# Half of the first MLP layer as a Strassen product, with its token sums on GpSimd

## The chip, the cores and the metric

The kernel runs on one core of one Trainium2 chip. The metric is the time of one execution on the device in microseconds (us); the runs of a kernel are given by their median. A profile shows one execution, taken by the hardware profiler. PE is TensorE (PEld its weight loads), DVE is VectorE, ACT is ScalarE, POOL is GpSimd, SP is SyncE, which here only issues DMAs.

## The reference

Attention with 4 sink tokens and a window of 128, on 4 batches, 8 heads, 768 positions and head size 64, then layer normalisation and a two-layer MLP with a residual, on tokens of 512 values and 2048 hidden units. All inputs and the output are f32.

```python
keep = is_sink | in_window
scores = np.where(keep, scale * q @ k.T, -1e9)
a = softmax(scores)
x = (a @ v) with the heads side by side          # 4 x 768 x 512
xn = (x - mu) / np.sqrt(var + 1e-6) * g_ln
out = x + np.maximum(xn @ w_ch1, 0.0) @ w_ch2    # 512 -> 2048 -> 512
```

## The kernel before, in words

**Work.** A chunk is 256 tokens (two tiles of 128), three to a batch, twelve in all. `chunk` loads q, k and v of a chunk and brings q and k into transposed form (`kq`), from the fifth chunk on by plain loads into `nat` on POOL's queue (L659) and DMA transposes on SP's queue (L660 with L551). `attend` makes the scores in two halves (matmuls L763), the exponentials on ACT (L777), the mask multiply on DVE (L781), and `value` the products with v (L800, L805). `value` goes on with the normalisation on DVE and POOL: reciprocal (L818), x (L820), its statistics (L824, L826), the inverse square root on POOL (L832, L833), the normalised tile xc (L835) and its DMA transpose into `xnt` on SP (L845).

**The MLP.** `mlp` makes the first layer of a chunk in eight blocks of 128 x 512 results, each of 8 matmuls with 256 columns (L880), that is two groups of 128 hidden units for 256 tokens. In the first two chunks a block has one tile of tokens and 16 matmuls with 128 columns (L873). ACT or DVE evicts a block with its relu (L890, L892) into `hq`. From the third chunk on the second layer is a Strassen-Winograd product in `wino`: sums of quarters of the hidden values on DVE (L943), seven products of 8 matmuls each (L960), and sums out of the banks on DVE (L974, L981). PSUM has two pairs of banks for the attention and four single banks (`one`) for everything else. Sums of w2's quarters are made once (L1029).

**Order.** Nothing is issued in the order of the text. Each step is put to a planner (`Plan.op`) with the engines that may do it, a cost on each and a priority in units of time (chunk c's MLP has T = 16 c + 8; the steps of its attention are offsets in `PAR`). `Plan.run` goes through time on its own model of the engines, picks the ready step with the lowest priority on the engine that is free first, and gives buffers of a ring (`nat`, `x`, `pe`, ...) as they come free. From 40 units on, TensorE's steps keep strictly to the order of their priorities. What comes out is one fixed list, issued under a manual schedule; on the chip each engine runs its share in that order and waits on semaphores where the data ask for it. POOL's queue holds both its arithmetic and its loads. A load of chunk c is tied to the square root of chunk c - 3 (`behind`).

```python
def behind(c):
    return [roots[2 * (c - 3) + 1]] if c >= PAR["behind"] else []
...
P.op(f"{nm}ld{c}{i}", {"POOL": (0.87, 0.9)}, ld + 0.01 * i + 0.1 * x,
     lambda e, nat=nat, ap=ap: G.dma_start(nat.t, ap), writes=[nat], dma=SW, after=behind(c))
```

Of the kernel before, what the change touches and what calls it, by code (L numbers as in the profile page):

```python
# [7 lines left out]
FP32 = mybir.dt.float32  # L8
# [56 lines left out]
class Plan:  # L65
# [6 lines left out]
    LANES = 8  # L72
    SHARED = 36.0

    def __init__(self):
# [37 lines left out]
    def run(self):  # L113
# [8 lines left out]
        while ready:  # L122
# [50 lines left out]
            if o.dma is None:  # L173
                o.end = st + lat
            else:
                busy, first, last = o.dma
                q = "POOL" if e == "POOL" else "HW"
                at = max(st + occ + first, dma_free[q], dma_free["all"] if st < self.SHARED else 0.0) + busy
                dma_free[q] = dma_free["all"] = at
                o.end = at + last  # L180
                lanes[q][n_dma[q] % self.LANES] = o.end
                n_dma[q] += 1
# [29 lines left out]
def fix(occ, extra=0.09):  # L212
    return (occ, occ + extra)
# [9 lines left out]
HW_T = (0.10, 0.8, 0.8)  # L223

LOW, HIGH = 1e-9, 1e9
NEG = -1e30
NEVER = -1e9

PAR = dict(split=(3, 4, 5, 6, 7), gsum=-8.0, guard=183.0, strict=40.0, win=0.4, tr=-8.0, sc=-5.3, sc1=-2.0, av=2.0, trx=9.0, by_dma=4, x_by_dma=2, g_on_w=2, av2=20.0, avi=1.0, behind=5, gtt=9.0, ramp=0.3, vs0=2.6, vpb=12.0,
           w1p=(0.15, 1.7, 2.05, 2.8), pm=2, w2p=(4.5, 4.51, 4.52, 4.53), by_tile=2, wino=2, vp=(0.0, 0.1, 2.0, 2.1, 4.2, 4.3), ld1=0.05)  # L230

# [130 lines left out]
def kernel(  # L362
# [12 lines left out]
    nc = tc.nc  # L375
# [21 lines left out]
    def ring(name, n, shape, dtype, pool=consts):  # L397
        P.ring(name, [Slot(pool.tile(shape, dtype, name=f"{name}{i}"), f"{name}{i}") for i in range(n)])
# [10 lines left out]
    ring("kq", 4, [128, HP, 2, 256], BF16)  # L409
    ring("pe", 12, [128, 2, 512], BF16)  # L410
    ring("ps", 3, [128, 256], BF16)
    ring("kts", 2, [128, HP, 32], BF16)
    ring("x", 16, [128, DM], BF16)
    ring("xc", 6, [128, DM], BF16)
    ring("xnt", 4, [128, NDM, 256], BF16)
    ring("hq", 8, [128, 4, 512], BF16)
    ring("hs", 10, [128, 2, 2, 128], BF16)
    ring("tm", 6, [128, 256], FP32)
    ring("ot", 4, [128, DM], FP32)
# [116 lines left out]
    def at(c, step):  # L536
        return 16.0 * c - 8.0 + PAR[step]

# [15 lines left out]

    def behind(c):
        return [roots[2 * (c - 3) + 1]] if c >= PAR["behind"] else []

    def load_v(t, prio):
        b, r = t // RB, t % RB
        bv = Buf(f"v{t}", "vn")  # L560
        vn_b[t] = bv
        P.op(f"vld{t}", {"POOL": (0.87, 0.9)}, prio, lambda e: G.dma_start(  # L562
            bv.t[:, :, 0:64], v[b, :, 128 * r:128 * (r + 1), :].rearrange("h p d -> p h d")),
            writes=[bv], dma=SW, after=list(ones_of.values()) + behind(t // 2))
# [13 lines left out]
    def chunk(c):  # L578
# [74 lines left out]
        else:  # L653
            for x, (nm, src) in enumerate((("k", k), ("q", q))):
                for i in range(2):
                    nat = Buf(f"{nm}n{c}{i}", "nat")
                    ap = src[b, :, 256 * R + 128 * i:256 * R + 128 * (i + 1), :].rearrange("h p d -> p h d")
                    P.op(f"{nm}ld{c}{i}", {"POOL": (0.87, 0.9)}, ld + 0.01 * i + 0.1 * x,
                         lambda e, nat=nat, ap=ap: G.dma_start(nat.t, ap), writes=[nat], dma=SW, after=behind(c))  # L659
                    P.op(f"tr{nm}{c}{i}", {"SP": (1.2, 1.2)}, d + 0.01 * i, lambda e, nat=nat, i=i, x=x: dma_t(  # L660
                        T.t[:, :, x, 128 * i:128 * i + 128], nat.t.rearrange("p h d -> p (h d)")),
                        reads=[nat], writes=[T], dma=HW_X, after=[scores[c - 1]])
# [75 lines left out]
    def attend(c):  # L738
# [48 lines left out]
        for i in range(2):  # L787
            def part(h, n, i=i):
                col = 256 * i + 128 * n if R else 128 * (i + n)
                return pes[h // 2].t[:, h % 2, col:col + 128]  # L790
            value(c, i, pes, ps, (PAR["av2"] if c == 2 else at(c, "av")) + PAR["avi"] * i, part, [2 * c + i - 1, 2 * c + i] if R or i else [2 * c])

    def value(c, i, pes, ps, d, part, srcs):
# [3 lines left out]
        def av(e):  # L797
# [5 lines left out]
            for h in range(H):  # L803
# [13 lines left out]
        recs.append(rcb)  # L817
        P.op(f"rc{t}", {"DVE": fix(0.115)}, d + 0.1, lambda e: V.reciprocal(rc(), pv()[:, :, :, 64]),  # L818
             reads=[po], writes=[rcb])
        P.op(f"x{t}", {"DVE": dve(512)}, d + 0.11, lambda e: V.tensor_tensor(  # L820
            x.t.rearrange("p (a h c) -> p a h c", a=2, c=64), pv()[:, :, :, 0:64],
            rc().unsqueeze(3).to_broadcast([128, 2, 4, 64]), op=ALU.mult), reads=[po, rcb], writes=[x])
        mv = Buf(f"mv{t}")
        P.op(f"bn{t}", {"DVE": fix(0.60)}, d + 0.12, lambda e: V.bn_stats(st.t[:, 8:14], x.t),  # L824
             reads=[x], writes=[st, mv])
        P.op(f"ag{t}", {"DVE": fix(0.09)}, d + 0.13, lambda e: V.bn_aggr(st.t[:, 14:16], st.t[:, 8:14]),  # L826
             reads=[st], rw=[mv])
        rs = Buf(f"rs{t}")
        xst_b[t, "rs"] = rs
        scaled = c >= PAR["wino"]  # L830
        roots[t] = P.op(f"rs{t}", {"POOL": (0.83, 0.88)}, d + (0.5 if scaled else 5), lambda e: (
            G.tensor_scalar(st.t[:, 17:18], st.t[:, 15:16], 1e-6, None, op0=ALU.add),  # L832
            G.tensor_tensor(st.t[:, 16:17], st.t[:, 17:18], mhalf, op=ALU.pow)),  # L833
            reads=[st, mv, Bc["mhalf"]], writes=[rs])
        P.op(f"xc{t}", {"DVE": fix(0.26)}, d + (0.6 if scaled else 0.14), lambda e: V.tensor_scalar(  # L835
            xc.t, x.t, st.t[:, 14:15], st.t[:, 16:17] if scaled else None, op0=ALU.subtract,
# [7 lines left out]
        if c >= PAR["x_by_dma"]:  # L844
            P.op(f"trx{t}", {"SP": (1.2, 1.2)}, d + 0.5, lambda e: dma_t(xnt_b[c].t[:, :, 128 * i:128 * i + 128], xc.t),  # L845
                 reads=[xc], writes=[xnt_b[c]], dma=HW_X)
            return
# [5 lines left out]
        if c >= PAR["g_on_w"]:  # L853
# [5 lines left out]
            reads=[pt, Bc["gt"]], writes=[xnt_b[c], xnt_t[t]])  # L859

    def mlp(c):
        T = 16.0 * c + 8.0
# [3 lines left out]
        hq = [Buf(f"hq{c}_{g}", "hq") for g in range(2)]  # L866
        for u in range(NH1 // 2):
            ph, hb, hg = Buf(f"ph{c}_{u}", "one"), Buf(f"h{c}_{u}"), hq[u // 4]
# [7 lines left out]
            def mm(e, u=u, ph=ph):  # L876
                for s in range(2):
                    ht = 2 * u + s
                    for j in range(NDM):
                        nc.tensor.matmul(ph.t[:, 256 * s:256 * s + 256],  # L880
                                         lhsT=w1[ht // 4][:, j, 128 * (ht % 4):128 * (ht % 4 + 1)],
                                         rhs=xnt.t[:, j, :], start=j == 0, stop=j == NDM - 1)
            pr = T + u + 0.5
            o = P.op(f"ph{c}_{u}", pe(0.872), pr, mm_t if by_tile else mm, reads=[xnt_t[2 * c + u % 2] if by_tile else xnt, (Bw1 if c < PAR["g_on_w"] else Bw1g)[u // 2]],
# [11 lines left out]
        if c >= PAR["wino"]:  # L896
            return wino(c, T, hq, h1)
        for i in range(2):
# [27 lines left out]

    def wino(c, T, hq, h1):
        A = [lambda g=g: hq[g].t.rearrange("p (v k) (s t) -> p k v s t", k=2, s=2) for g in range(2)]
        part = {"a11": lambda g: A[g]()[:, 0, :, :, 0:128], "a21": lambda g: A[g]()[:, 0, :, :, 128:256],
                "a12": lambda g: A[g]()[:, 1, :, :, 0:128], "a22": lambda g: A[g]()[:, 1, :, :, 128:256]}  # L930
        deps = {n: [h1[4 * g + (0 if n[2] == "1" else 1)::2][:2] for g in range(2)] for n in part}
        sb = {}
# [6 lines left out]
        for i, (n, x0, x1, op) in enumerate((("s3", "a11", "a21", ALU.subtract), ("s1", "a21", "a22", ALU.add),  # L939
                                             ("s2", "s1", "a11", ALU.subtract), ("s4", "a12", "s2", ALU.subtract))):  # L940
            for g in range(2):
                sb[n, g] = Buf(f"{n}_{c}{g}", "hs")
                P.op(f"{n}_{c}{g}", {"DVE": dve(512, 0.52)}, T - 4 + 4 * g + 0.2 * i, lambda e, n=n, x0=x0, x1=x1, g=g, op=op: V.tensor_tensor(  # L943
                    sb[n, g].t, get(x0, g), get(x1, g), op=op),
                    reads=need(x0, g) + need(x1, g), writes=[sb[n, g]], hold=[hq[g]])
# [25 lines left out]
        def keep(name, r, done, half, pr):  # L971
            tm[name] = Buf(f"tm{name}{c}", "tm")
            i, sl = half // 2, slice(256 * (half % 2), 256 * (half % 2) + 256)
            return P.op(f"tm{name}_{c}", {"DVE": dve(256, 1.14)}, pr, lambda e: V.tensor_tensor(  # L974
                tm[name].t, at(r), xs[i].t[:, sl], op=ALU.add), reads=[done, xs[i]], hold=[bank[reg[r][0]]], writes=[tm[name]])
        oo = {}

        def final(r, done, name, half, pr):
            i, sl = half // 2, slice(256 * (half % 2), 256 * (half % 2) + 256)
            oo[half] = Buf(f"oo{c}{half}")  # L980
            return P.op(f"o{c}_{half}", {"DVE": dve(256, 1.14)}, pr, lambda e: V.tensor_tensor(  # L981
                ots[i].t[:, sl], at(r), tm[name].t, op=ALU.add), reads=[done, tm[name]], hold=[bank[reg[r][0]]], writes=[ots[i], oo[half]])
# [49 lines left out]

    for c in range(NC):
        mlp(c)
        if c == PAR["g_on_w"] - 1:
# [93 lines left out]
```

## Time and profile before

| what | value |
|---|---|
| three runs shown | 210.74, 211.32, 211.52 us (median 211.32) |
| the profiled execution's own time | 211.71 us |
| its span, first to last instruction | 210.2 us |
| PE, DVE, ACT, POOL busy | 203.0, 162.2, 114.1, 83.5 us |
| granted TensorE clock | 1.000 |
| chain that ended last | PE 90%, DMA 3%, DVE 3%, POOL 2% |
| matmuls of layer one, L880 | 640, 74.5 us busy |
| matmuls of layer two, L960 | 320 with `hs`, 240 with `hq` weights |

The span is what the trace covers; about 1.5 us lie around it. Matmuls run in a pipeline: a row's mean (273 ns for L880) is the time from start to finish of one, while the next starts after 109 ns, so a block's length is read from the chain or the timeline and not from the mean. On DVE and ACT a queued instruction starts about 0.1 us before the one ahead has ended. A group's idle time is what its engine waited just before it.

### The profile page before, as it was taken

To read this page: it belongs to the slowest core of one execution; us is meant where nothing else is said; L and a number is where in the kernel's file an instruction comes from. 1 tells how busy PE (TensorE), PEld (TensorE's weight loads), DVE (VectorE), ACT (ScalarE), POOL (GpSimd) and SP (SyncE) were. 2 spreads that over 40 slices of the span, in tenths; PEclk is the share of its full clock that TensorE was granted. 3 is DMA by queue.
4 is the path that set the end of the run, shared out by engine and by line. 5 is a ranking of instruction groups with operands and counts; after the bars stand their busy time and mean duration, and the time that the engine had idled before them with its cause. 6 is when DMAs were issued, how large, how long until landed. Compare 5 with 4: busy or idle time off the path is not lost.

```text
span 210.2 us, 6259 instructions
## 1 busy us (share of the span) xinstructions
PE 203.0 (97%) x2539; PEld 167.9 (80%) x2544; DVE 162.2 (77%) x410; ACT 114.1 (54%) x168; POOL 83.5 (40%) x126
## 2 busy tenths in 40 slices
PE   6978999999999999999999999999999999999994
PEld 2657997764787997997987987987988988988883
DVE  5579759999688688798687797797787786797353
ACT  2559479837564564564556555554457457450620
POOL 7967583369058057058066066066020020020000
PEclk9999999999999999999999999999999999999999
DMA  5999999999999949939959939939954520220202
GB/s 115 156 198 191 199 191 208 189 173 154 212 167 127 172 109 136 188 78 120 166 122 150 174 79 156 172 77 151 177 100 53 150 53 3 100 50 4 103 30 83
DMA packets 101243, 27.51 MB, mean 131 GB/s; under 512 B 89556, under 2 KB 99032, under 8 KB 101208
## 3 DMA queue, kind: packets, MB, share of 16 engines
q0 software_dynamic: 67712, 13.37, 77.7%
q1 hardware_dynamic: 33208, 13.41, 35.5%
q8 instruction: 21, 0.34, 0.7%
q10 hardware_dynamic: 288, 0.26, 0.4%
q14 instruction: 14, 0.11, 0.2%
HBM read 27.30 MB, written 6.29 MB: 160 GB/s over the span
## 4 chain that ended last, share of the span: by engine, by line
PE 90%; DMA 3%; DVE 3%; POOL 2%; issue 0%; DVEq 0%
PE one L880 33%; PE one L960 30%; PE one L873 7%; PE one L911 7%; PE pair L805 5%; PE pair L763 4%; DMA n4b<-in_q_dram 3%; PE pair L800 2%; PE one L645 1%; POOL nat L599 1%; PE one L767 1%; DVE xnt L857 1%; DVE kq L568 1%; POOL vn L562 0%; DVE st L824 0%
## 5 line engine op out<-in xcount | busy, mean ns | idle before, releaser
L890 ACT ACTIVATE hq<-one 128x512 bf16<-128x512 f32 x92 | 55.0, 597 | 55.7 <-PE one L880 46.7
L880 PE MATMUL one<-xnt,w 128*128 128x256 bf16 x640 | 74.5, 273 | 0.0
L880 PEld LDWEIGHTS <-w 128*128 128x128 bf16 x640 | 61.4, 98 | 7.0
L777 ACT ACTIVATE pe<-pair 128x1024 bf16<-128x1024 f32 (+1 forms) x40 | 36.2, 960 | 23.2 <-PE pair L763 19.0
L832 POOL TENSOR_SCALAR st<-st 128x1 f32<-128x1 f32 x24 | 6.2, 259 | 88.2 <-DVE rec L818 74.6
L960 PEld LDWEIGHTS <-hs 128*128 128x128 bf16 x320 | 30.0, 98 | 5.2 <-DVE tm L974 0.3
L974 DVE TENSOR_TENSOR tm<-one,x 128x256 f32<-128x256 f32 x40 | 16.9, 422 | 12.3 <-PE one L960 12.3
L781 DVE TENSOR_TENSOR pe<-pe,mask 128x1024 bf16<-128x1024 bf16 (+1 forms) x40 | 24.9, 644 | 1.0 <-ACT pe L777 0.8
L960 PEld LDWEIGHTS <-hq 128*128 128x128 bf16 x240 | 23.5, 98 | 2.7
L562 POOL DMA_DIRECT2D vn<-in_v_dram x24 | 21.8, 922 | 2.0 <-DMA w<-in_moe_w_ch_dram 1.1
L943 DVE TENSOR_TENSOR hs<-hq 128x512 bf16<-128x512 bf16 x40 | 15.4, 413 | 5.3 <-ACT hq L890 5.2
L960 PE MATMUL one<-w,hq 128*128 128x256 bf16 x160 | 19.1, 273 | 0.0
L981 DVE TENSOR_TENSOR ot<-one,tm 128x256 f32<-128x256 f32 x40 | 16.7, 418 | 1.1 <-PE one L960 0.9
L820 DVE TENSOR_TENSOR x<-pair,rec 128x512 bf16<-128x512 f32 x24 | 16.6, 691 | 0.8
L824 DVE BATCH_NORM_STATS2 st<-x 128x6 f32<-128x512 bf16 x24 | 16.6, 692 | 0.5
L873 PE MATMUL one<-xnt,w 128*128 128x128 bf16 x256 | 16.3, 219 | 0.5 <-DVE xnt L857 0.5
L873 PEld LDWEIGHTS <-w 128*128 128x128 bf16 x256 | 14.7, 98 | 1.6 <-issue 0.5
L659 POOL DMA_DIRECT2D nat<-in_k_dram x16 | 15.0, 938 | 2.5 <-DMA w<-in_moe_w_ch_dram 2.5
L659 POOL DMA_DIRECT2D nat<-in_q_dram x16 | 14.2, 898 | 3.4 <-DMA w<-in_moe_w_ch_dram 3.4
L833 POOL TENSOR_TENSOR st<-st,mhalf 128x1 f32<-128x1 f32 x24 | 14.2, 592 | 2.0
L911 PE MATMUL one<-w,hq 128*128 128x512 bf16 x60 | 14.8, 380 | 0.2
L805 PE MATMUL pair<-vn,pe 128*128 128x65 bf16 x352 | 14.6, 193 | 0.0
(113 smaller groups left out, 245.1 us busy)
## 6 DMA issues: line engine op xcount, KB each, us to landing
out_dram<-ot SPq DMA_DIRECT2D x17, 256.0 KB
w<-in_moe_w_ch_dram POOLq DMA_DIRECT2D x8, 512.0 KB, 12.6
vn<-in_v_dram POOLq DMA_DIRECT2D x24, 128.0 KB, 7.2
nat<-in_k_dram POOLq DMA_DIRECT2D x17, 128.0 KB, 4.8
nat<-in_q_dram POOLq DMA_DIRECT2D x17, 128.0 KB, 5.3
out_dram<-ot SPq DMA_DIRECT2D x14, 128.0 KB
kq<-nat SPq DMA_TRANSPOSE x32
xnt<-xc SPq DMA_TRANSPOSE x20
```

What stands on the lines that cost most here:

```text
L562: P.op(f"vld{t}", {"POOL": (0.87, 0.9)}, prio, lambda e: G.dma_start(bv.t[:, :, 0:64], v[b, :, 128 * r:128 * (r + 1), :].rearrange("h p d ...
L659: lambda e, nat=nat, ap=ap: G.dma_start(nat.t, ap), writes=[nat], dma=SW, after=behind(c))
L777: P.op(f"ex{c}{hp}", {"ACT": act(2 * n)}, d + 0.1 + 0.05 * j, lambda e, pp=pp, pb=pb: nc.scalar.activation(pb.t[:, :, 0:n], pp.t[:, :, 0:n ...
L781: V.tensor_mul(pb.t[:, :, 0:n], pb.t[:, :, 0:n], mm),
L805: nc.tensor.matmul(po.t[:, h // 4, 65 * (h % 4):65 * (h % 4) + 65], lhsT=part(h, n), rhs=vn_b[tv].t[:, h, :], start=(not R and h % 4 == 0 ...
L873: nc.tensor.matmul(ph.t[:, 128 * s:128 * s + 128], lhsT=w1[u // 2][:, j, 128 * s:128 * s + 128], rhs=xnt.t[:, j, 128 * (u % 2):128 * (u % ...
L880: nc.tensor.matmul(ph.t[:, 256 * s:256 * s + 256], lhsT=w1[ht // 4][:, j, 128 * (ht % 4):128 * (ht % 4 + 1)], rhs=xnt.t[:, j, :], start=j ...
L890: nc.scalar.activation(hg.t[:, u % 4, :], ph.t, AF.Relu)
L911: nc.tensor.matmul(pc.t[:, 0:wd], lhsT=(hq[s // 2].t[:, (2 * s + i) % 4, 128 * ii:128 * ii + 128] if by_tile else hq[ht // 8].t[:, ht // 2 ...
L960: nc.tensor.matmul(at(r), lhsT=get(left, g)[:, v, s, :], rhs=rhs, start=first and n == 0, stop=n == 7, skip_group_check=True)
L974: return P.op(f"tm{name}_{c}", {"DVE": dve(256, 1.14)}, pr, lambda e: V.tensor_tensor(tm[name].t, at(r), xs[i].t[:, sl], op=ALU.add), read ...
L981: return P.op(f"o{c}_{half}", {"DVE": dve(256, 1.14)}, pr, lambda e: V.tensor_tensor(ots[i].t[:, sl], at(r), tm[name].t, op=ALU.add), read ...
```

## The change

Chunks 4 to 11 (`half=4`, counted from 0) make the first four of the eight blocks of layer one, the 1024 hidden units of w1's first two tiles, as a Strassen-Winograd product: a 2 x 2 split of the weights (units by inner dimension) and of the tokens (inner dimension by tile). The four sums of weight quarters are made once on DVE (`weight_sums`), into two buffers of the `hq` ring that stay taken. The four sums of token quarters of each chunk are made on POOL, 128 x 256 each, from `xnt` into a new ring `xt`. Seven products of 8 matmuls with 128 columns run in three banks. Partial results are copied by ACT into a new ring `tz` of f32, added to a bank by DVE into `hq`, and the relu is done in place by ACT; the last quarter is evicted with its relu directly. The other four blocks, and layer two, keep their form.

The offsets of the attention's steps, of the second layer's sums and of the DVE work behind the value matmuls get new values from chunk 5 on (`h=dict(...)`, `sp`, `sq`, `kp`); the steps stand in other places in the lists for that reason too. Ring `pe` goes from 12 to 10 buffers and `x` from 16 to 12; `nat` keeps its 8. `soon`, `lb` and `rd` are 0, and with `MIXED = 1e9` the planner's other branch for DMAs isn't entered. In the list that comes out, POOL has the token sums of a chunk behind the six loads that follow the chunk's square roots, and TensorE has, in a steady chunk: product 1, a second-layer product, product 2, the value matmuls of the next chunk, products 5 and 6, block 5, products 3 and 7, blocks 4 and 6, product 4, block 7, the first half of the scores, four second-layer products, the second half of the scores, two second-layer products.

```diff
-    ring("pe", 12, [128, 2, 512], BF16)
+    ring("pe", 10, [128, 2, 512], BF16)
-    ring("x", 16, [128, DM], BF16)
+    ring("x", 12, [128, DM], BF16)
+    ring("xt", 2, [128, 4, 2, 128], BF16)
+    ring("tz", 2, [128, 512], FP32)
...
     def at(c, step):
-        return 16.0 * c - 8.0 + PAR[step]
+        return 16.0 * c - 8.0 + (PAR["h"] if c > PAR["half"] else PAR)[step]
...
+    def weight_sums():
+        a = [w1[m][:, 2 * i:2 * i + 2, :] for m in range(2) for i in range(2)]
+        get = {n: (lambda i=i: a[i]) for i, n in enumerate(("a11", "a12", "a21", "a22"))}
+        held = [Buf(f"ws{i}", "hq") for i in range(2)]
+        for i, (x0, x1, op) in enumerate((("a21", "a22", ALU.add), (0, "a11", ALU.subtract),
+                                          ("a11", "a21", ALU.subtract), ("a12", 1, ALU.subtract))):
...
+            P.op(f"wsum{i}", {"DVE": dve(1024, 0.52)}, PAR["wsum"] + 3.0 * i, lambda e, ap=ap, x0=x0, x1=x1, op=op, val=val:
+                 V.tensor_tensor(ap(), val(x0), val(x1), op=op), reads=Bw1g[0:2] + [wsum[x][1] for x in (x0, x1) if isinstance(x, int)],
+                 hold=[held[i // 2]], writes=[done], nb=PAR["wsum"] + 3.0 * i)
...
+    def halves(c, T, hq):
+        xnt = xnt_b[c]
+        f = PAR["flip"]
+        B = {f"b{i + 1}{j + 1}": (lambda i=i, o=128 * (j ^ f): xnt.t[:, 2 * i:2 * i + 2, o:o + 128]) for i in range(2) for j in range(2)}
+        sums = Buf(f"xt{c}", "xt")
...
+        for i, (n, x0, x1) in enumerate((("t0", "b12", "b11"), ("t2", "b22", "b12"), ("t1", "b22", "t0"), ("t3", "b21", "t1"))):
+            got[n] = Buf(f"x{n}_{c}")
+            last_xt = P.op(f"xt{n}_{c}", {e: dve(256, 0.52) if e == "DVE" else fix(0.72) for e in PAR["te"]}, T - PAR["tlead"] + 0.1 * i, lambda e, n=n, x0=x0, x1=x1: (V if e == "DVE" else G).tensor_tensor(
+                right(n), right(x0), right(x1), op=ALU.subtract), reads=[xnt] + [got[x] for x in (x0, x1) if x[0] == "t"],
+                hold=[sums], writes=[got[n]])
...
+        def product(i, bank, left, rt, first, after=()):
+            b, done = banks_[bank], Buf(f"m{i}_{c}")
+
+            def mm(e):
+                lt = a[left]() if isinstance(left, str) else wsum[left][0]()
+                rh = right(rt)
+                for h in range(4):
+                    for kk in range(2):
+                        nc.tensor.matmul(b.t[:, 128 * h:128 * h + 128], lhsT=lt[:, kk, 128 * h:128 * h + 128], rhs=rh[:, kk, :],
+                                         start=first and h == 0 and kk == 0, stop=kk == 1, skip_group_check=True)
...
+        def snap(i, bank, done):
+            tz = Buf(f"tz{i}{c}", "tz")
+            o = P.op(f"tz{i}_{c}", {"ACT": act(512)}, T + pos[i - 1] - PAR["tzp"], lambda e: nc.scalar.copy(tz.t, banks_[bank].t),
+                     reads=[done], hold=[banks_[bank]], writes=[tz])
+            return tz, o
...
+        def total(n, bank, done, tz, pr):
+            raw, outs[n] = Buf(f"raw{n}{c}"), Buf(f"{n}_{c}")
+            o = P.op(f"c{n}_{c}", {"DVE": dve(512, 1.14)}, pr, lambda e: V.tensor_tensor(
+                block(n), banks_[bank].t.rearrange("p (i t) -> p i t", i=4), tz.t.rearrange("p (i t) -> p i t", i=4), op=ALU.add),
+                reads=[done, tz], hold=[banks_[bank], hq], writes=[raw])
+            P.op(f"r{n}_{c}", {"ACT": act(512), "DVE": dve(512, 0.26)} if PAR["rd"] else {"ACT": act(512)}, pr + 0.1, lambda e: nc.scalar.activation(block(n), block(n), AF.Relu) if e == "ACT" else
+                 V.tensor_scalar_max(block(n), block(n), 0.0), reads=[raw], hold=[hq], writes=[outs[n]])
+            return o
...
+        m1 = product(1, "z", "a11", "b11", True)
+        t1, o1 = snap(1, "z", m1)
+        m5 = product(5, "y", 0, "t0", True)
+        t5, o5 = snap(5, "y", m5)
+        m2 = product(2, "w", "a12", "b21", True)
+        total("c11", "w", m2, t1, T + pos[1] - late_)
+        m6 = product(6, "z", 1, "t1", False, [o1])
+        t2, o2 = snap(6, "z", m6)
+        m3 = product(3, "y", 3, "b22", False, [o5])
+        total("c12", "y", m3, t2, T + pos[5] - late_)
+        m7 = product(7, "z", 2, "t2", False, [o2])
+        o3 = total("c22", "z", m7, t5, T + pos[6] - late_)
+        m4 = product(4, "z", "a22", "t3", False, [o3])
...
-        for u in range(NH1 // 2):
+        strassen = c >= PAR["half"]
+        quick = halves(c, T, hq[0]) if strassen else None
+        for u in range(4 if strassen else 0, NH1 // 2):
...
-            pr = T + u + 0.5
+            pr = T + (PAR["pos4"][u - 4] if strassen else u + 0.5)
```

## The prediction

> **What bounds the kernel now.** I read the page's head and slices first, then the chain of waits in order of time, then who waits for whom, then busy time in a stretch of the steady state, then the rows of what the change touches.
>
> ```profile
> span 210.2 us, 6259 instructions
> ...
> PE 203.0 (97%) x2539; PEld 167.9 (80%) x2544; DVE 162.2 (77%) x410; ACT 114.1 (54%) x168; POOL 83.5 (40%) x126
> ...
> PE   6978999999999999999999999999999999999994
> ...
> PEclk9999999999999999999999999999999999999999
> ```
>
> TensorE is busy from the third slice on at the full granted clock. The chain of waits in order of time (start, length, what) says that it waits for nobody:
>
> ```profile
> 21.64 0.89 PE one L873 x16
> ...
> 116.56 1.75 PE one L880 x16
> 118.31 0.22 PE pair L800 x2
> 118.53 0.48 PE pair L805 x16
> 119.02 0.87 PE one L880 x8
> ...
> 124.97 1.75 PE one L960 x16
> 126.71 0.46 PE pair L763 x24
> ```
>
> From 62 us to the last product at 207 us no wait of TensorE is listed, so what it is spared comes off the end, as long as every other engine keeps up. A chunk period (L880 block to L880 block) is 15.88 us with 24 score matmuls, 15.6 and 15.2 around a first chunk of a batch. VectorE is the next engine; the columns here are stretch, its length, then busy us of PE, PEld, DVE, ACT, POOL:
>
> ```profile
> 85.00:180.00 95.00, 95.00 (x1169) 82.29 (x1168) 76.67 (x189) 52.06 (x77) 31.47 (x48) 1.00 1.11 119
> ```
>
> DVE idles 18.3 us in these six periods, 3.05 us a period; ACT idles 7 us a period.
>
> **What the change removes and adds on TensorE.** In chunks 4 to 11 the first half of layer one was 4 blocks of 8 matmuls of 256 columns: L880 x8 lasts 0.87, so 3.49 us. It becomes 7 products of 8 matmuls of 128 columns. Such matmuls, with a new weight tile each, stand in L873: 16 in 0.89 us, 55.6 ns each, 0.445 a product, 3.12 us for seven. Saved: 0.37 a chunk, **3.0 us** over 8 chunks. The upper bound of the new price is L873's slowest group without a wait of its own (64 in 3.72 us, 58 ns): 3.25, saved 1.9. I take 55.6, since the 58 holds one pause of 0.13.
>
> The Trainium skill (TensorE: Matmul & The Clock Gate, Back-to-back issue gap) speaks against this: it gives about 81 ns per matmul for a stream of weight load and 128-column matmul. By it seven products would take 4.54 us, the change would lose 8.4 us and end at 219.7. This trace has 55.6 ns for just that stream.
>
> **ACT.** Eight evictions a chunk (L890, 0.597) become three snapshots, one relu eviction and three evictions of the other half, plus three relus in place. Bounds of the last, which stands in no row: 0.597 (L890) and 0.758 (L1039, SBUF to SBUF, 128x512); I take the upper. 7 x 0.597 + 3 x 0.758 = 6.45 against 4.78: 1.7 more, inside the 7 idle. Three products wait for a snapshot (a bank goes on only when it has been copied). The built order behind the value matmuls is product 5, product 6, block 5, products 3 and 7, blocks 4 and 6, product 4, block 7. The tightest is product 7, which starts 1.77 us after product 5's end; two snapshots in a row need 0.16 (matmul tail, 0.273 less 0.109), 0.09 from PE's end to ACT's start, 0.48 from start to start, 0.60 and 0.1 back to PE: 1.43. Slack 0.34. No cost; if ACT is late by more, it falls on TensorE one to one.
>
> **DVE.** Three sums of a bank and a snapshot, 128x512 out of f32:
>
> ```profile
> L781 DVE TENSOR_TENSOR pe<-pe,mask 128x1024 bf16<-128x1024 bf16 (+1 forms) x40 | 24.9, 644 | 1.0 <-ACT pe L777 0.8
> ...
> L820 DVE TENSOR_TENSOR x<-pair,rec 128x512 bf16<-128x512 f32 x24 | 16.6, 691 | 0.8
> ```
>
> 0.691 each, 0.61 from start to start when queued. One eviction of the other half now stands on DVE too (L892, 0.60). Together 3 x 0.61 + 0.60 = 2.43 a chunk. Of 3.05 idle that leaves 0.62, less the 0.37 by which the chunk shrinks: **0.25 us**. About eight idle gaps a chunk each hide a tail of 0.08 that a queued DVE does not pay, so at most 0.85 is left. I take the middle, 0.55. Four weight sums (128x1024, 0.60 each) come once, two chunks earlier: no cost. The order gives two handoffs with little slack. Between the last score matmul and the value matmuls stand three second-layer products and two new ones, 3.5 us, for two exponentials and the last mask multiply (0.1 + 0.90 + 1.02 + 0.05 + 0.68): slack 0.7. And product 4 waits for the third sum, queued behind both tiles' normalisation: it starts 4.0 us after product 5's end, the sum ends about 3.6 after it: slack 0.4. Behind chunk 11's attention no scores stand among chunk 10's second-layer products any more, so its DVE sums are due 0.9 us (two score stretches of 0.46) sooner: I add a third of it, 0.3, once.
>
> **POOL and the queues.** Four token sums a chunk stand behind the six loads and in front of the next tile's square root. They wait for both xnt transposes; behind them only that square root waits, and
>
> ```profile
> POOL st L832 <- DVE rec L818: 74.6, 10, 12.7
> ```
>
> 7.5 us a chunk are free there. On SP the fourth kq transpose moves behind a second store; it is used over 5 us later (in the trace it is issued at 118.9 and its scores start at 126.7; scores move up by two products, 1.75 us). Loads are issued in the same order behind the same root. Smaller pe and x rings still hold 2.5 and 6 chunks. No cost. A POOL sum of 2 x 256 elements has no row: from below, the select of 128 elements (L463, 0.294) less the one-element op (L832, 0.222) is 0.56 ns an element, 512 reads and the fixed 0.222 make 0.51; from above, the planner's own occupancy and completion in the diff, 0.72 + 0.09 = 0.81. I take 0.66.
>
> What such a sum does to DVE is the open price. Beside each other, the two engines hold each other up (lines of two stretches of the timeline, then durations min/median/max of a line):
>
> ```profile
> 17.44 0.68 DVE L720 TENSOR_TENSOR pe<-pe,mask 128x1024 bf16<-128x1024 bf16 x1
> ...
> 17.71 0.85 POOL L833 TENSOR_TENSOR st<-st,mhalf 128x1 f32<-128x1 f32 x1
> ...
> 93.40 1.87 POOL L659 DMA_DIRECT2D nat<-in_k_dram  x2
> ...
> 94.48 0.80 DVE L666 COPY kts<-kq 64x16 bf16<-64x16 bf16 x2
> ```
>
> ```profile
> L666 DVE COPY kts<-kq x8: 157/309/624, 8.0 to 141.3; 64x16 bf16<-64x16 bf16 x8
> ...
> L833 POOL TENSOR_TENSOR st<-st,mhalf x24: 568/572/854, 15.0 to 186.2; 128x1 f32<-128x1 f32 x24
> ```
>
> The square root beside a mask multiply took 854 instead of 572 ns. The second copy of kts took 624 instead of 157 and ended with POOL's load at 95.27. Beside L820, whose input is in PSUM, POOL took its usual 568. So a sum that reads SBUF may hold a DVE multiply of two SBUF operands (masks, second-layer sums: 4 x 0.60 + 8 x 0.335 = 5.1 us of a 15.5 us chunk) for its reading time, 0.66 less the 0.22 fixed: 0.44. Bounds a chunk: nothing, or 4 x 0.59 = 2.4 (all four hit, at 0.81). By share of time DVE loses 4 x 0.44 x 0.33 = 0.58; the sums come beside the second pair of mask multiplies, so I take 0.77. Less 0.55 idle: 0.22 a chunk reach TensorE, 1.5 us over the seven chunks whose sums have an attention beside them. The trace does not show DVE held by an arithmetic POOL instruction of any size.
>
> The Trainium skill (SBUF — State Buffer, Who interferes with whom) has the rule: VectorE copies in a two-port mode contend with GpSimd, two SBUF inputs on VectorE contend with a GpSimd instruction that reads SBUF, and whoever starts first holds the shared pair for all of its instruction. Both slow rows agree with it. The Trainium skill's GpSimd page (GPSIMD Engine Reference, Elementwise — side-by-side cycle accounting) has 2.6 cycles an element at 1.2 GHz, an estimate of 0.56 us for 256; by that alone the held time would be 0.55 and DVE's loss by share 0.7.
>
> **Sum** against the profiled execution's 211.71 (span 210.2, 1.5 around it): -3.0 + 0.3 + 1.5 = -1.2, 210.5. The three runs shown have their median 0.39 lower, at 211.32; a measurement is a median, so I predict **210.1**.
>
> **Rivals.**
> 1. The cover holds (DVE is not held, or its idle time takes it up): -3.0 + 0.3, **208.6**. For it: no TensorE wait in 145 us today, and slack at every new handoff. Against: 0.25 to 0.85 us of DVE idle a chunk is little.
> 2. Slower: DVE becomes the bound through the shared port. Place: mask multiplies and second-layer sums beside the token sums. Price 0.44 to 0.59 per hit. It turns the sign when the loss a chunk passes the idle time plus 2.7/7 = 0.39, that is 0.64 to 1.24 us, two of four sums. Three hits at 0.59 are 1.77, less 0.55, 1.2 x 7 = 8.5: **217**; two hits of 0.59 with 0.25 idle, 0.93 x 7 = 6.5: 215; just past the point 212.5. For it: both slow rows. Against: DVE's other two thirds leave gaps in which the sums fit.
> 3. The change moves nothing visible: the stalls eat 2 to 3.5 us, **210.6 to 212.3**.
> 4. 128-column matmuls bound by their weight loads: at PEld's 0.098 us (mean of one, not overlapped) 56 cost 5.5 us, 2.0 a chunk more, 16 in all: **227**. Against: the 55.6 ns of L873, whose weights are new each time too. The Trainium skill's figure of the back-to-back section is the milder form of this rival.
>
> **Chances.** Forecast with stalls of 0.7 to 2.0 us (209.3 to 210.6) 0.35; rival 1 (208.3 to 209.3) 0.22; rival 3 0.17; rival 2 0.24; rival 4 0.02. Half a per cent, 1.06 us, is about what a measurement of this kernel can tell from no change (the three runs spread 0.4%): faster 0.45 (rival 1 and two thirds of the forecast), same 0.29, slower 0.26. Range: from rival 1's 208.4 to 214, which cuts off the worse part of rival 2 and rival 4. The forecast's own range is 209.3 to 210.6.
>
> **What would show it.** Right: eight matmuls of the products (line 934 of the changed kernel) in 0.44 us; chunk periods of 15.5 where they were 15.88; DVE over 93% busy in 85 to 180 us; the token sums (line 914, on POOL) 0.5 to 0.8 us, and mask multiplies of over 1 us beside it. Wrong: TensorE waits on ACT (snapshots late), on a transpose, or none; product matmuls over 60 ns; waits on DVE of over 0.5 us a chunk, with the mask multiplies and second-layer sums stretched (rival 2).

## The result, and the profile after

The changed kernel takes **213.22 us** (median of ten runs, 212.39 to 214.57) against 211.35 for the kernel before (ten runs): a ratio of 1.0094, interval 1.0068 to 1.012. It is slower by 0.9 per cent; the forecast was 210.1, faster. One run of e9 below took 284.45 us at a granted clock of 0.685 and is left out of that kernel's median.

The page of the changed kernel, head, engines and slices; the profiled execution took 212.39 us:

```profile
span 210.9 us, 6718 instructions
...
PE 201.3 (95%) x2731; PEld 167.6 (79%) x2736; DVE 182.9 (87%) x447; ACT 119.6 (57%) x183; POOL 109.9 (52%) x158
...
PE   6989999999999999999999999999998999998991
```

TensorE is busy for 1.7 us less (203.0 before), and yet the span is 0.7 us longer. Busy time between 85 and 180 us (stretch, length, PE, PEld, DVE, ACT, POOL), and TensorE's list of waits between 60 and 206 us, both of the changed kernel:

```profile
85.00:180.00 95.00, 94.21 (x1345) 82.84 (x1343) 90.27 (x216) 56.32 (x90) 54.21 (x75) 1.00 1.10 121
```
```profile
PE one L1085 <- DVE tm L1099: 1.4, 3, 0.6
```

DVE went from 76.67 to 90.27 us, 95% of the stretch, and TensorE now waits for it. What DVE loses stands in the timeline. First DVE, then POOL, beside the first pair of mask multiplies of chunk 10 (start, length of the group, what, how many):

```profile
155.41 0.75 DVE L1068 TENSOR_TENSOR hs<-hq 128x512 bf16<-128x512 bf16 x2
...
157.08 2.13 DVE L806 TENSOR_TENSOR pe<-pe,mask 128x1024 bf16<-128x1024 bf16 x2
159.14 0.41 DVE L1099 TENSOR_TENSOR tm<-one,x 128x256 f32<-128x256 f32 x1
159.47 0.41 DVE L1106 TENSOR_TENSOR ot<-one,tm 128x256 f32<-128x256 f32 x1
```
```profile
156.93 1.74 POOL L914 TENSOR_TENSOR xt<-xnt 128x256 bf16<-128x256 bf16 x2 [3.49 <-DMA xnt<-xc]
158.63 1.86 POOL L914 TENSOR_TENSOR xt<-xnt,xt 128x256 bf16<-128x256 bf16 x2
```

Two mask multiplies that take 1.28 us by themselves take 2.13, and four token sums of 0.66 take 3.6. They take turns here: a mask multiply waits for the token sum that came first, the next token sum for the mask multiply. L1099 and L1106, whose first operand is in PSUM, have their usual 0.41 beside the same sums. TensorE's product that needs the bank freed by L1099 waits 0.62 us for it and starts at 159.60. In the whole trace only lines with two SBUF operands are stretched by token sums, L806 by 2.85 us, L1068 by 1.63 and the single row L1172, beside chunk 11's sums, by 0.35 (357 ns in e1 below):

```profile
L806 DVE TENSOR_TENSOR pe<-pe,mask x40: 544/680/1161, 33.4 to 177.4; 128x1024 bf16<-128x1024 bf16 x28, 128x768 bf16<-128x768 bf16 x12
```
```profile
L1068 DVE TENSOR_TENSOR hs<-hq,hs x20: 392/416/1731, 60.9 to 203.0; 128x512 bf16<-128x512 bf16 x20
```
```profile
L1172 DVE TENSOR_TENSOR low<-low,rec x1: 706/706/706, 189.7 to 189.7; 128x192 f32<-128x192 f32 x1
```
```profile
L914 POOL TENSOR_TENSOR xt<-xnt x16: 659/806/1607, 83.0 to 188.9; 128x256 bf16<-128x256 bf16 x16
```

That is not all. TensorE's last matmul starts 0.9 us earlier than before, 206.57 (L1182) against 207.47 (L1055), and the span ends 0.7 us later. What happens behind it stands in the rows of the closing branch, at which every engine jumps over code that this input does not need. Kernel before, then changed kernel (sequencer instructions; duration, then first and last start):

```profile
L1089 DVEq COMPARE_BRANCH  x1: 72/72/72, 207.6 to 207.6; - x1
...
L1089 DVEq EVENT_SEMAPHORE  x1: 21/21/21, 208.2 to 208.2; - x1
```
```profile
L1216 DVEq COMPARE_BRANCH  x1: 72/72/72, 206.7 to 206.7; - x1
...
L1216 DVEq EVENT_SEMAPHORE  x1: 21/21/21, 209.8 to 209.8; - x1
```

DVE's first instruction behind its branch comes 0.6 us after it in the kernel before and 3.1 us after it in the changed one, and the last barrier of all engines, whose longest wait on SP goes from 28 to 1833 ns, waits for DVE. Kernel before, then changed kernel:

```profile
L1124 SPq EVENT_SEMAPHORE  x14: 17/28/28, 208.3 to 210.1; - x14
```
```profile
L1251 SPq EVENT_SEMAPHORE  x14: 17/28/1833, 207.5 to 210.8; - x14
```

The executions can be laid side by side at two marks of TensorE, the first score matmul of chunk 4, which the change does not move, and the last matmul of all:

| kernel | first mark | last matmul | between | behind it |
|---|---|---|---|---|
| before | 64.09 | 207.47 | 143.38 | 2.7 |
| changed | 63.49 | 206.57 | 143.08 | 4.3 |
| e1: token sums left out | 63.49 | 204.55 | 141.06 | 4.2 |
| e3: hint for DVE | 63.83 | 207.14 | 143.31 | 2.7 |
| e4: token sums added to before | 64.12 | 207.91 | 143.79 | 2.7 |
| e7: before, DVE filled | 63.36 | 206.75 | 143.39 | 4.2 |
| e9: sums behind the masks | 63.58 | 205.34 | 141.76 | 4.3 |
| e10: the same and hint | 63.62 | 205.31 | 141.69 | 2.7 |
| e11: sums left out and hint | 64.14 | 205.31 | 141.17 | 2.7 |

Before to changed: -0.6 at the start (which varies by 0.8 between kernels that are alike up to there), -0.3 between the marks, +1.7 behind them (2.68 and 4.34 before rounding).

### The profile page after: what moved, and what is told of

Its sections match the earlier page's. It is cut to its first block, busy times and chain, and to the rows that moved or that the text cites. A ratio compares the mean times of both kernels' runs of the same rounds, so it can differ in the third digit from the quotient of the medians.

```text
span 210.9 us, 6718 instructions
## 1 busy us (share of the span) xinstructions
PE 201.3 (95%) x2731; PEld 167.6 (79%) x2736; DVE 182.9 (87%) x447; ACT 119.6 (57%) x183; POOL 109.9 (52%) x158
## 5 line engine op out<-in xcount | busy, mean ns | idle before, releaser
L1003 PE MATMUL one<-xnt,w 128*128 128x256 bf16 x384 | 46.8, 273 | 0.0
L1013 ACT ACTIVATE hq<-one 128x512 bf16<-128x512 f32 x51 | 30.2, 596 | 19.8 <-PE one L1003 10.3
L1003 PEld LDWEIGHTS <-w 128*128 128x128 bf16 x384 | 36.3, 98 | 3.9
L1085 PEld LDWEIGHTS <-hs 128*128 128x128 bf16 x320 | 30.8, 98 | 5.0 <-issue 1.3
L806 DVE TENSOR_TENSOR pe<-pe,mask 128x1024 bf16<-128x1024 bf16 (+1 forms) x40 | 27.2, 715 | 0.9 <-ACT pe L802 0.8
L959 ACT ACTIVATE hq<-hq 128x512 bf16<-128x512 bf16 x24 | 14.9, 630 | 21.1 <-DVE hq L956 21.1
L1085 PEld LDWEIGHTS <-hq 128*128 128x128 bf16 x240 | 22.4, 98 | 4.7 <-issue 1.2
L914 POOL TENSOR_TENSOR xt<-xnt 128x256 bf16<-128x256 bf16 x16 | 14.1, 902 | 15.3 <-DMA xnt<-xc 15.3
L945 ACT COPY tz<-one 128x512 f32<-128x512 f32 x24 | 13.2, 583 | 14.1 <-PE one L934 13.9
L1106 DVE TENSOR_TENSOR ot<-one,tm 128x256 f32<-128x256 f32 x40 | 16.1, 414 | 2.5 <-PE one L1085 1.9
L1099 DVE TENSOR_TENSOR tm<-one,x 128x256 f32<-128x256 f32 x40 | 16.6, 416 | 1.4 <-PE one L1085 1.0
L1068 DVE TENSOR_TENSOR hs<-hq 128x512 bf16<-128x512 bf16 x40 | 15.5, 419 | 1.8 <-ACT hq L1013 1.3
L996 PEld LDWEIGHTS <-w 128*128 128x128 bf16 x256 | 14.7, 98 | 2.0 <-issue 0.5
L859 POOL TENSOR_TENSOR st<-st,mhalf 128x1 f32<-128x1 f32 x24 | 15.2, 632 | 2.0
L850 DVE BATCH_NORM_STATS2 st<-x 128x6 f32<-128x512 bf16 x24 | 15.9, 685 | 0.2
```

Source lines behind the costliest of these rows:

```text
L806: V.tensor_mul(pb.t[:, :, 0:n], pb.t[:, :, 0:n], mm),
L850: P.op(f"bn{t}", {"DVE": fix(0.60)}, d + xo + 0.12, lambda e: V.bn_stats(st.t[:, 8:14], x.t), reads=[x], writes=[st, mv])
L996: nc.tensor.matmul(ph.t[:, 128 * s:128 * s + 128], lhsT=w1[u // 2][:, j, 128 * s:128 * s + 128], rhs=xnt.t[:, j, 128 * (u % 2):128 * (u % ...
L1003: nc.tensor.matmul(ph.t[:, 256 * s:256 * s + 256], lhsT=w1[ht // 4][:, j, 128 * (ht % 4):128 * (ht % 4 + 1)], rhs=xnt.t[:, j, :], start=j ...
L1013: nc.scalar.activation(hg.t[:, u % 4, :], ph.t, AF.Relu)
L1068: P.op(f"{n}_{c}{g}", {"DVE": dve(512, 0.52)}, T - PAR["sp"][g] + PAR["sq"][i], lambda e, n=n, x0=x0, x1=x1, g=g, op=op: V.tensor_tensor(s ...
```

## The experiments

Theory A: the token sums on POOL hold DVE's instructions of two SBUF operands, and DVE has no idle time left where it would be needed. Theory B: DVE's own additional work is too much, with or without the holding. Theory C: DVE stands still behind the closing branch because the code at its target has not been fetched, which depends on where the branch and its target lie in DVE's program, and so on the number of instructions ahead of them. Each run was timed beside the kernel before (211.28 to 211.33 us).

**e1, token sums left out.**

```diff
...
-                right(n), right(x0), right(x1), op=ALU.subtract)
+            G.memset(sums.t[:, int(n[1]), 0, 0:1], 0.0)
```

> The changed kernel with its four token sums a chunk replaced on POOL by four one-element writes; the products read unsummed quarters of xnt (so the token sums are left out of the computation). Same instructions and same order on TensorE, DVE, ACT and SP. Theory A (shared port: the POOL sums hold DVE): mask multiplies never over 0.70 us, second-layer sums never over 0.45, DVE idle in 85 to 180 us rises from 4.7 to 8.5 to 10 us, TensorE's waits from 62 us to the last product fall from 1.9 us to under 0.6, and the median falls by 1.5 to 2.8 us, to 210.4 to 211.7. Theory B (DVE's own 2.43 us a chunk are too much, the hold does not matter): waits stay over 1.3 us, median 212.5 to 213.3. Theory C (the 3.0 us in which DVE stands still behind the closing branch): stays as it is here, since DVE has the same instructions.

Measured: 210.7 us, 2.5 less than the changed kernel (ratio to before 0.9992, interval 0.9974 to 1.0011). No mask multiply is over 0.69 us. Mask multiplies, busy time between 85 and 180 us, and TensorE's waits:

```profile
L806 DVE TENSOR_TENSOR pe<-pe,mask x40: 546/682/693, 33.4 to 175.5; 128x1024 bf16<-128x1024 bf16 x28, 128x768 bf16<-128x768 bf16 x12
```
```profile
85.00:180.00 95.00, 95.00 (x1368) 84.50 (x1366) 88.58 (x219) 58.20 (x92) 32.67 (x72) 1.00 1.11 125
```
```profile
PE one L1182 <- DVE ot L1106: 0.5, 1, 0.5
PE one L1085 <- DVE tm L1099: 0.2, 1, 0.2
```

The first is the end that every version has. The chunk periods (first scores of one chunk to those of the next) are 15.51 and 14.56 us where the kernel before has 15.88 and 14.93: 0.37 less each. Between the marks e1 is 2.02 us shorter than the changed kernel. So A and not B: DVE is busy for 88.58 of 95 us here, nearly as much as with the token sums, and holds up TensorE by 0.2 us in one place. The idle time was less than expected (6.4 us, not 8.5 to 10); the 4.2 us behind the last matmul stay, as C said.

**e2, token sums on DVE.**

```diff
-te=("POOL",)
+te=("DVE",)
```

> The four token sums go from POOL to DVE. Each should take about 0.25 us there (estimate: the 128x512 sums of line 1068 take 0.42 and start every 0.335 when queued), 0.8 us a chunk. Theory A: no mask multiply over 0.70 us; what DVE gets back (4.5 us of holding in the whole profile, 0.6 a chunk) and what it takes on (0.8) are nearly equal: median 212.8 to 214.0. Theory B: an engine with 0.75 us idle a chunk gets 0.8 us more, and the median rises to 214 to 217. Theory C: DVE has 16 rows more, so the standstill behind the closing branch may be another one than 3.0 us.

Measured: 225.18 us (the profiled execution took 227.65), outside what either theory gave. No mask multiply is over 0.70 us and a sum takes 0.28, but the planner put them into DVE's queue ahead of second-layer sums, where they wait for the transposes of xnt. DVE's list of waits, then TensorE's:

```profile
DVE xt L914 <- DMA xnt<-xc: 4.6, 4, 2.8
```
```profile
PE one L1085 <- DVE tm L1099: 5.4, 5, 3.0
PE one L1085 <- DVE hs L1068: 4.8, 6, 1.2
```

The run does not tell A from B; it shows what waits at the head of DVE's queue cost. My expectation had left the queue out.

**e3, a branch hint for DVE**, one instruction at the start of its program that names the place of the branch.

```diff
-    tc.mark_branch_hint_location("all_is_well", engines=[mybir.EngineType.PE])
+    tc.mark_branch_hint_location("all_is_well", engines=[mybir.EngineType.PE, mybir.EngineType.DVE])
```

> The changed kernel with a branch hint for DVE beside the one for TensorE, nothing else. Theory C (behind the closing branch DVE waits for code that has not been fetched): the 3.0 us between DVE's branch and its next instruction fall to about the 0.5 us of the kernel before, what comes behind TensorE's last matmul falls from 4.2 to about 2.5 us, and the median by 1.4 to 2.0 us, to 211.2 to 211.8. Rival (the standstill is a delay of that one execution or belongs to the flag's load): no change, 212.8 to 213.6. Theories A and B: mask multiplies of 1.1 us beside the token sums and TensorE waits of 1.5 to 3 us stay as they are.

Measured: 212.05 us, 1.17 less than the changed kernel (ratio 1.0048, interval 1.003 to 1.0066). The branch and what follows it:

```profile
L1216 DVEq COMPARE_BRANCH  x1: 84/84/84, 207.3 to 207.3; - x1
...
L1216 DVEq EVENT_SEMAPHORE  x1: 21/21/21, 207.9 to 207.9; - x1
```

0.6 us again, and 2.7 behind the last matmul. The middle is as in the changed kernel, 143.31. C stands; the median gained a little less than expected.

**e4, token sums added to the kernel before.**

```diff
...
+        for i in range(4 if c >= 4 else 0):
+            P.op(f"idle{i}_{c}", {"POOL": fix(0.72)}, T - 28.07 + 0.1 * i, lambda e: G.tensor_tensor(
+                extra, xnt.t[:, 0:2, 0:128], xnt.t[:, 2:4, 128:256], op=ALU.subtract), reads=[xnt], hold=[xnt], nb=T + 8.0)
```

> The kernel before with four POOL sums of 128x256 a chunk from the fifth chunk on, of the same form and at the same place in POOL's queue as those of the change, into a buffer that nobody reads; the order on every other engine is as before. Theory A: mask multiplies of 0.9 to 1.2 us where such a sum stands beside them, 3 to 5 us of stretching on DVE in all, hidden by its 3.05 us of idle time a chunk: median 211.2 to 212.0, DVE idle in 85 to 180 us down from 18.3 to 13 to 16 us. Theory B (no holding): all DVE lines at their old durations, median 211.1 to 211.6.

Measured: 211.45 us against 211.33, a ratio of 1.0009 (0.9995 to 1.0022). The holding is there in full, mask multiplies (L782 in this kernel) stretched by 4.97 us:

```profile
L782 DVE TENSOR_TENSOR pe<-pe,mask x40: 548/682/1372, 34.0 to 179.6; 128x1024 bf16<-128x1024 bf16 x28, 128x768 bf16<-128x768 bf16 x12
```

With 3 us idle a chunk it costs 0.4 us between the marks, where a second-layer sum of chunk 10 is held (0.40, TensorE 0.38 late). It is the same holding as in the changed kernel, and as much of it. What differs is how much DVE idles where its readers wait; the two kernels' orders differ too, so that this alone sets the price is argued, not shown.

**e5 and e6, sums behind the masks, first attempt.**

```diff
...
-                hold=[sums], writes=[got[n]])
+                hold=[sums], writes=[got[n]], after=[last_mask[c + 1]] if c + 1 in last_mask else [])
```

> The changed kernel, all of it, with one more wait: the four token sums of a chunk start on POOL only when the last mask multiply of the next chunk's attention is done. What stands beside them on DVE then reads a PSUM bank (second-layer sums of banks, lines 1099 and 1106, and the totals, line 956). TensorE's and DVE's order is unchanged. Theory A (a POOL sum holds only DVE instructions with two SBUF operands): no mask multiply over 0.75 us, token sums 0.66 us each, TensorE's listed waits from 60 us under 0.7 us, median near that of the kernel without the sums: 210.5 to 211.5. Rival (the later sums come too late for products 5 and 6, which stand 2 us behind the masks): TensorE waits for POOL 0.1 to 0.6 us a chunk, median 211.5 to 213.5. Rival (POOL sums hold DVE whatever it reads): lines 1099, 1106 and 956 stretched by 0.2 us and more, median 212.5 to 213.5.

> The kernel of the run before this one with the branch hint for DVE as well. Theories A and C add up: 1.2 to 1.6 us under that run, 209.0 to 210.2, faster than the kernel before by 0.5 to 1.1 per cent. If C is an effect of chance, no difference to that run.

Measured: 214.46 us (ratio 1.0149, interval 1.0115 to 1.0182) and, with the hint, 212.58 (1.0071, interval 1.0043 to 1.01). The edit did not do what it was meant to: `after` tells the planner an order between engines but puts no semaphore into the program, so the token sums started beside the masks as before (stretched L808 and L1070 by 4.8 us in e5). What the pair still shows is the hint, 1.9 us. That e5's median lies 1.2 above the changed kernel's, with the same time between the marks to 0.2 us, is not explained.

**e7, the kernel before with 63 more instructions on DVE.**

```diff
...
+    for i in range(63):
+        P.op(f"fill{i}", {"DVE": fix(0.06)}, 5000.0 + i, lambda e: V.memset(spare, 0.0), nb=150.0 + 0.8 * i)
```

> The kernel before with 63 one-element writes on DVE into a spare tile, spread over the last 50 us, in which DVE has idle time. DVE's program then has as many instructions ahead of the closing branch as in the changed kernel (537 instead of 474, its waits counted). Nothing else is changed. Theory C (where the closing branch and its target lie in DVE's program decides whether the target's code has to be fetched): DVE stands still for about 3.0 us behind its branch instead of 0.5, the time behind TensorE's last matmul goes from 2.65 to about 4.2 us, median 212.5 to 213.3. Rival (the standstill comes from something else in the change, its buffers or its semaphores): 0.5 us as before, median 211.3 to 211.8.

Measured: 213.26 us against 211.28, ratio 1.0093 (1.0057 to 1.0129). TensorE is not touched, 143.39 between the marks where the kernel before has 143.38, and yet:

```profile
L1092 DVEq COMPARE_BRANCH  x1: 72/72/72, 206.9 to 206.9; - x1
...
L1092 DVEq EVENT_SEMAPHORE  x1: 21/21/21, 209.9 to 209.9; - x1
```

3.0 us behind the branch, 4.2 behind the last matmul. Nothing but the number of DVE's instructions was changed: the standstill belongs to that, as C said. The instruction packets between 206 and 211 us point the same way. Kernel before, then changed kernel:

```profile
q14 instruction: 2, 0.02, 1.1%
```
```profile
q14 instruction: 3, 0.02, 2.0%
```

Each is a block of 8192 bytes. In the trace's record of single packets the additional one starts at 210.40 us, 0.6 us after DVE went on. Wherever an engine stands still behind this branch there is one block more, and the engine goes on 1.0 to 1.5 us after the block that follows its branch has landed. Which code a block holds is not on record.

POOL and ACT show the same standstill, and it costs nothing there because they jump 6 us and more ahead of DVE: ACT's next instruction comes 2.45 us after its branch in the kernel before and 2.73 in the changed one, POOL's 2.67 and 0.47. So on POOL it is the longer program that does not stand: e4, which adds token sums and their waits to POOL and nothing to the other engines, takes POOL from 185 to 225 instructions ahead of the branch and from 2.67 to 0.47 us. What counts is where the branch and its target lie, not that a program is long.

**e8, the kernel before with the hint of e3.**

> The kernel before with the branch hint for DVE, nothing else. Theory C: the target's code is there already (0.5 us behind the branch), so the hint brings nothing: median 211.1 to 211.6. If a hint saves time by itself, it is under 211.

Measured: 211.36 us against 211.28 (ratio 1.0005, 0.9988 to 1.0022). The hint brings nothing where DVE does not stand still without it.

**e9 and e10, sums behind the masks with a true wait; e10 has e3's hint as well.**

```diff
...
+        turn = Buf(f"turn{c}")
+        if c + 1 in last_masked:
+            pb = last_masked[c + 1]
+            P.op(f"turn{c}", {"POOL": fix(0.2)}, T - PAR["tlead"] - 0.1, lambda e: G.tensor_copy(turn_t, pb.t[:, 0, 0:1]),
+                 reads=[pb], writes=[turn])
...
-reads=[xnt] + [got[x] for x in (x0, x1) if x[0] == "t"],
+reads=[xnt] + ([turn] if c + 1 in last_masked else []) + [got[x] for x in (x0, x1) if x[0] == "t"],
```

> The changed kernel with one more POOL instruction a chunk ahead of the token sums: a copy of one element of the last masked tile of the next chunk's attention, so that the sums cannot start before the last mask multiply is done (the run e5 meant to do this, but its wait was only in the planner's list, and the sums started as before). Theory A: no mask multiply over 0.75 us and no second-layer sum over 0.5, token sums of 0.66 us, TensorE's chunk periods 15.51 and 14.56 us as in the kernel without the sums, median 210.4 to 211.3 (that kernel: 210.7). Rival 1 (the sums come too late for products 5 and 6): periods 15.7 to 16.1, TensorE waiting for POOL, median 211.5 to 213.5. Rival 2 (POOL's sums hold every DVE instruction that touches SBUF): lines that read PSUM stretched by 0.2 us and more, periods as in the changed kernel, median 212.5 to 213.5.

> The run before this one with the branch hint for DVE. If A and C both hold they add up: 1.2 to 1.6 us under that run, 209.0 to 209.9, faster than the kernel before by 0.6 to 1.1 per cent. If the sums come too late: 210 to 212.

Measured: e9 211.69 us (ratio 1.0019, 0.9999 to 1.0039), 1.5 less than the changed kernel and 0.4 over the upper end of what A gave. In its trace mask multiplies (L809 there), second-layer sums and token sums (L923) have their usual lengths again:

```profile
L809 DVE TENSOR_TENSOR pe<-pe,mask x40: 548/681/692, 33.5 to 176.0; 128x1024 bf16<-128x1024 bf16 x28, 128x768 bf16<-128x768 bf16 x12
```
```profile
L923 POOL TENSOR_TENSOR xt<-xnt x16: 657/666/670, 85.4 to 187.7; 128x256 bf16<-128x256 bf16 x16
L923 POOL TENSOR_TENSOR xt<-xnt,xt x16: 659/668/680, 86.6 to 189.1; 128x256 bf16<-128x256 bf16 x16
```

The sums stand beside L1108, L1115, L965 and L850 now, which have a PSUM operand, and hold none of them. TensorE waits for POOL nowhere, and most periods are 15.51 and 14.56. One row is still held, beside chunk 11's sums, which have no attention behind them and so no wait:

```profile
L1181 DVE TENSOR_TENSOR low<-low,rec x1: 705/705/705, 188.5 to 188.5; 128x192 f32<-128x192 f32 x1
```

TensorE waits 0.57 us behind it where it waits 0.22 in e1. That is half of the 0.70 us by which e9 is longer than e1 between the marks. The other 0.34 lies inside the scores that start at 123.28, where a weight load waits for nothing that the profile shows; its cause is open.

e10 is at **209.78 us** (ratio 0.9928, interval 0.9901 to 0.9955), 1.9 under e9, more than the 1.2 to 1.6 expected, and 3.4 under the changed kernel: 0.7 per cent faster than the kernel before.

**e11, token sums left out (as in e1) and the hint (as in e3).**

> The changed kernel with the token sums left out of the computation (four one-element writes in their place, as in e1) and the branch hint for DVE: what the change would be worth without the holding and without the standstill. From 211.3: 8 x 0.37 saved is 3.0, chunk 10's second layer gives back 0.6 (measured in e1): 209.0, 208.7 to 209.5. If e1's and the hint's gains overlap: 210.0 to 210.7.

Measured: 209.44 us (ratio 0.9901, interval 0.9876 to 0.9925). The two effects add up. e10 is 0.3 us above it in medians and 0.5 between the marks; the row that is still held there accounts for some 0.35 of it (TensorE waits 0.6 us behind it in e10, 0.2 in e11).

## Why the prediction was wrong, point by point

In medians the balance is: from the kernel before to e11 -1.87 (211.31 to 209.44), what the Strassen product is worth by itself; from e11 to e3 +2.61, the holding; from e3 to the changed kernel +1.17, the standstill. Together +1.91, and measured is +1.87. In the traces of e1, the changed kernel and e3 the same three are -2.3, +2.0 and +1.7; the execution of e3 that was profiled took 211.28, near the fastest of its twelve, so the two accounts need not agree more closely.

- **TensorE's saving, 3.0.** Right. A product of eight matmuls lasts 0.45 us, and each of the eight chunks is 0.37 us shorter as soon as nothing waits. Its signs came as named: DVE at 95% of the stretch, and mask multiplies of over 1 us beside the token sums. The 81 ns a matmul of the Trainium skill (TensorE: Matmul & The Clock Gate, Back-to-back issue gap) would have made the chunks longer; the trace has 56 ns for it, and the measurement decides. Rival 4 fell with it.
- **ACT, no cost.** Right: TensorE waits for ACT in none of these traces.
- **Chunk 10's second layer, 0.3.** Too small: TensorE's starts are 0.24 and 0.38 us late there in e1, 0.62 in all.
- **The token sums, 0.66 us on POOL, and 0.44 a hit.** Right in the main: 0.66 undisturbed, and the eight held mask multiplies are 0.14 to 0.48 longer, 0.36 in the mean. DVE's loss was put at 0.77 a chunk; it is 4.48 us in seven chunks, 0.64, and 0.35 more on L1172 beside chunk 11's sums, which the prediction had left out. The rule of the Trainium skill that the prediction used (SBUF — State Buffer, Who interferes with whom) agrees with which rows are stretched, and e9 bears it out from the other side: beside instructions with a PSUM operand nobody is held, and its one held row has two SBUF operands. Its order, by which whoever starts first goes first, does not fit one row: L1068 at 112.83 us started before the second and the third token sum beside it (112.94 and 113.56) and came through behind both.
- **What of it reaches TensorE, 1.5.** Too small: 2.0 in the trace, 2.6 in medians. The step that failed here is "Less 0.55 idle". Without the holding DVE idles 6.42 us in the six chunks of e1's stretch, 1.07 a chunk, more than the 0.55, more than its upper bound of 0.85 and more than the loss of 0.64; by that subtraction nothing would have reached TensorE. With the holding DVE still idles 0.79 a chunk (95 less 90.27, over six), but not in front of the sums for which TensorE stands ready, so holding and idle time do not cancel. In e4, with three microseconds of idle time a chunk, nearly all of it is hidden.
- **The end, nothing.** This step failed too, and it is as large as the one before. The sum was made "against the profiled execution's 211.71 (span 210.2, 1.5 around it)" as if all that lies behind TensorE's last matmul stayed as it was, and the change put 63 instructions more on DVE ahead of its closing branch. That costs 1.2 us by the median of e3, 1.7 in the traces, 2.0 in e7. Without it the changed kernel is at 212.05, in what the prediction called rival 3.
- **Which of the two turned the sign.** In the traces it is the end: ahead of it the saving is still 0.3 us larger than the loss. By the medians the holding alone does it, since e3 is above the kernel before (ratio 1.0048, interval 1.003 to 1.0066). Of the 3.1 us between the forecast change, -1.2, and the measured +1.87, the standstill is 1.2, the holding 1.1 (2.6 for 1.5) and the saving 0.8 (1.87 where 2.7 stood); of that last part 0.3 is chunk 10's second layer, and the rest stays open.
- **Rival 2** named the shared port, and its range holds the measured time. But its mechanism by itself, which "turns the sign when the loss a chunk passes the idle time plus 2.7/7 = 0.39", gives 212.05; its 212.5 and more were reached with the help of the standstill, of which it says nothing. That 213.22 lies inside the stated range, 208.4 to 214, is owed to that, and is luck.

The Trainium skill has a rule that fits the standstill (Runtime: NRT & Kernel Launch, Instruction fetch mechanics): code is fetched ahead in order, and a taken branch whose target is not in the part already fetched waits for the transfer. e3, e7 and e8 agree with it, and so do the packets. DVE does not stand with 474 instructions, waits counted, ahead of this branch and does with 537; no run has a number between, and POOL's case shows that more instructions can also end a standstill.

## What to carry to other kernels

In these runs a sum on POOL was free only as long as DVE's instructions beside it read PSUM, or DVE had idle time right in front of what TensorE waits for: look at which instructions stand beside each other, and if the wrong ones do, shift POOL by a wait of its own (e9). A branch at the end of the program belongs into every sum that changes an engine's number of instructions, up or down; read the row behind the branch, and try a hint for the engine that jumps last (e3, e10). And an order that a planner knows is not yet a wait that the chip knows: look for the moved instruction in the trace before its run is read.

## What was not expected of the hardware

- Holding goes both ways: beside two mask multiplies four token sums took 3.6 us instead of 2.7 (e9), and one sum took 1.61. It does not always take turns: where four sums followed each other without a gap (112.31 to 115.09 us), a second-layer sum of 0.42 us took 1.73 and so came through only behind the third.
- Sixty-three one-element writes of 59 ns on an engine with idle time cost 2.0 us (213.26 against 211.28), none of it in the place where they stand.
- Thirty-two more sums and their waits took a standstill away from POOL behind the same branch (2.67 us before, 0.47 in e4), where 63 more writes brought one to DVE.
